# Two more chunks attended in 64x64 quarters, and the first group's FFN2 placed ahead of the third group's FFN1

## The chip, the core and the metric

The kernel runs on one core of a Trainium2 chip. Its engines each work through a queue of their own: TensorE (PE; its weight loads are shown as PEld), VectorE (DVE), ScalarE (ACT), GpSimd (POOL) and SyncE (SP), which here only issues DMAs; GpSimd issues some too. The metric is the device time of one execution in microseconds; before and after are compared by the median of several runs.

## The reference, cut to what matters

Two stages. The first is an mLSTM cell over 4 batches x 8 heads, 768 steps, head size 40, written as a recurrence:

```python
m_new = maximum(f[t] + m, i[t]);  f_stab = exp(f[t] + m - m_new);  i_stab = exp(i[t] - m_new)
C = f_stab * C + i_stab * outer(v[t], k[t])      # per batch and head, 40 x 40
n = f_stab * n + i_stab * k[t]
y[t] = sigmoid(o[t]) * (C @ q[t]) / maximum(abs(n . q[t]), 1.0)
```

The second is a feed-forward layer on the 3072 tokens, each of 8 x 40 = 320 numbers: `relu(x @ w_in)**2 @ w_out`, with w_in 320 x 2048 and w_out 2048 x 320. The weights come as 64-bit floats and are turned into 32-bit ones in the kernel. All arithmetic is 32-bit floating point.

## The kernel before, in words

**Tiling.** The sequence of each batch is cut into 6 chunks of 128 steps; the 24 chunks of the four batches are counted through as s = 0 to 23, so chunks 0 to 5 are batch 0. Within a chunk the recurrence is written as attention: scores of 128 keys against 128 queries for 8 heads, weighted by exp(A + b), where A (broadcast from DRAM into `A_bc`) and b come from the gates. Between chunks a state C per head pair is carried on (`C_old` for the first chunks, `C_b` after). Two chunks make a group g of 256 tokens for the feed-forward layer: FFN1 gives 2048 hidden rows (`g2`), FFN2 the 320 outputs.

**Two forms of attention.** `attend` (L609) uses full 128x128 tiles: the products `hi` (old state), `dC` (new state) and `hp` (values), then `normalise` (L805), then `turn_rows` (L843), which transposes the result on TensorE into `xT`, the FFN's input. `attend_begin` (L684) and `attend_end` (L743) use 64x64 quarters of the array: `values_of_C` (L702), `values_of_P` (L717), `new_C` (L732). Between the halves stands a marker: a VectorE instruction on one element (L700) that waits for the first half on TensorE and for which the second half's `new_C` (or `values_of_C`) waits in turn. The quarter form gives its numerators transposed; they are turned in 32x32 blocks on VectorE (L758), stored to DRAM (`store_num`, `num_rows`), loaded rearranged (`load_num`), normalised (`normalise_turned`, L783), stored (`store_rows`, `x_rows`), loaded (`load_rows`) and turned by VectorE into `xT` (`turn_squares`, L838). It also needs the queries scaled by exp(A): `decays` (L480) on ScalarE and `scale_q` (L669) on VectorE.

The constants `KQ_SQ, X_SQ, ROT = 7, 6, 8` (L339) say from which chunk on the keys and queries are loaded in squares (`load_squares`, `turn_kq`), from which on x goes by DRAM, and from which on heads and keys are rotated.

**Order.** Everything is written out by hand; each engine works in the order of the program. First comes a prologue with the gates and chunks 0 and 1. Then a loop over u = 0 to 7 (L1228) does, on even u, scores and FFN1 quarters, and on odd u `attend(s)` for s = 2 to 5, the transposes of the next chunk, and another FFN1 quarter. Quarters 0 to 3 are FFN1 of group 0, quarters 4 to 7 of group 1. In between, `rounding` converts 18 pieces of the weights: `words` on ScalarE, `join` on VectorE with a last sum on GpSimd (L240), after which SP fetches the next raw piece. Pieces 0 to 9 are w_in, 10 to 17 w_out.

Then comes the main loop over `parts` (L1317), four parts n to a chunk from s = 6 on. In each set of four, part at = 0 has the scores, at = 1 `attend_begin`, the scores of the next chunk or FFN rows, `attend_end`, the stores and loads; at = 2 and 3 the steps on the next chunk. Each part carries a piece of FFN1 (which = 1: `ffn1_open`, `ffn1_rows`, `ffn1_close`, which trade multiplications for sums on VectorE, among them `xs`, `sums_of_x`, L1028) or FFN2 (which = 2). The parts begin with FFN1 of group 2 (`ffn1_begin`, L1046), then FFN2 of group 0 (`ffn2`, L906, four parts), then FFN2 of group 1, FFN1 of group 3, and so on; sums of w_out (`sums_of_weights`, T0 to T3, L935 to L946) serve the FFN2 of later groups (`ffn2_fast`).

PSUM: `ps_at` has 3 banks; in the u loop `ps_h` has 3 and `ps_o` 2, later `ps_h` has all 5.

Of the kernel before, what the change touches and what calls it, by code (L numbers as in the profile page):

```python
# [29 lines left out]
def kernel(  # L30
# [80 lines left out]
    bdm = conv.tile([P, PR, 2, D1], F32, bufs=1)  # L111
# [13 lines left out]
    def make_consts():  # L125
# [24 lines left out]
        nc.gpsimd.memset(bdm[:], 1.0)  # L150
        nc.gpsimd.memset(bdm[:DP, :, 1, :], 0.0)
        nc.gpsimd.memset(bdm[DP:, :, 0, :], 0.0)
# [186 lines left out]
    KQ_SQ, X_SQ, ROT = 7, 6, 8  # L339
# [22 lines left out]
    def load_k(s):  # L362
# [3 lines left out]
        eng = nc.sync if s < 10 else nc.gpsimd  # L366
# [4 lines left out]
    def load_v(s):  # L371
# [3 lines left out]
        eng = nc.sync if s < 10 else nc.gpsimd  # L375
# [88 lines left out]

    def mask(s):
# [14 lines left out]
    def decays(s):  # L480

        if s % NB > 0:
            e = st[s]["eA"] = kq_b[2 + s % 2][:, 1].rearrange("p (j two) d -> p j (two d)", two=2)
# [10 lines left out]
    def weigh(s, masked=False, part=None, vw=True):  # L494
# [4 lines left out]
        if s < X_SQ and part != 1:  # L499
            d["dec"] = prep.tile([P, H], F32, name="dec")  # L500
# [7 lines left out]
        for i in (range(len(A) if s < ROT else 0) if part is None else (part,)):  # L508
# [5 lines left out]
            if s < X_SQ:  # L514
                nc.scalar.activation(d["dec"][:, hh], A[i][:, :, P - 1], AF.Exp)
# [83 lines left out]
    C_old = []  # L599

    def decay_old(s):
        if s + 1 < NB:
            Cd = st[s]["Cd"] = old.tile([P, PR, 2, D1], F32, name="Cd", bufs=1)
            nc.gpsimd.tensor_tensor(
                Cd[:].rearrange("p j i d -> p (j i) d"), C_old[(s - 1) % 2][:].rearrange("p j i d -> p (j i) d"),
                st[s]["dec"][:].unsqueeze(2).to_broadcast([P, H, D1]), op=ALU.mult,
            )

    def attend(s):  # L609
# [41 lines left out]
        if c > 0:  # L651
            num = d["num"] = old.tile([P, H, D1], F32, name="num", bufs=1)
            nc.vector.tensor_tensor(
                num[:], hi[:], eA_T[:, b, c, :].unsqueeze(2).to_broadcast([P, H, D1]), op=ALU.mult,
# [3 lines left out]
        if c + 1 < NB:  # L658
            Cn = C_old[s % 2]
            if c == 0:  # L660
                nc.vector.tensor_tensor(Cn[:], dC[:], bdm[:], op=ALU.mult)
# [12 lines left out]
    def decay_C(s):  # L674
        if s % NB > 0:
            Cd = st[s]["Cd"] = attn.tile([P, PR, D1], F32, name="Cd", bufs=1)
            nc.gpsimd.tensor_tensor(
                Cd[:], C_b[(s - 1) % 2][:, : PR * D1].rearrange("p (j d) -> p j d", d=D1),
# [3 lines left out]
    LIVE = [slice(DP * i, DP * i + D) for i in range(2)]  # L682

    def attend_begin(s):  # L684
# [13 lines left out]
        else:  # L698
            end, spare = out[1][DP : DP + 1, P : P + 1], C_b[(s - 1) % 2][0:1, 4 * D1 : 4 * D1 + 1]
        nc.vector.tensor_scalar(spare, end, scalar1=0.0, scalar2=None, op0=ALU.mult)  # L700

    def values_of_C(s, rows, order=(0, 1)):  # L702
        d = st[s]
        C = C_b[(s - 1) % 2]
        for e in order:
            for m in order:
                i, j = rows[m], 2 * m + e
                nc.tensor.matmul(  # L708
                    d["numT"][m][HALVES[e], i, :], lhsT=C[LIVE[i], j * D1 : j * D1 + DP], rhs=d["eA"][LIVE[i], j, :],
# [33 lines left out]
    def attend_end(s):  # L743
# [11 lines left out]
        tn = attn.tile([P, P // SQ, PR, SQ], F32, name="tn", bufs=1)  # L755
        to = tn[:].rearrange("p m c r -> p c m r")
# [3 lines left out]
        if c + 1 < NB:  # L760
            Cn = C_b[s % 2][:, : PR * D1].rearrange("p (m x) -> p m x", m=2)
            for m in range(2):
                dC = d["out"][m][:, 2 * P : 2 * P + 2 * D1]
                if c > 0:
                    nc.vector.tensor_tensor(
                        Cn[:, m], dC, d["Cd"][:].rearrange("p (m e) d -> p m (e d)", m=2)[:, m], op=ALU.add,
# [5 lines left out]
    def store_num(s):  # L772
        nc.sync.dma_start(n_d[s], st[s]["tn"][:].rearrange("p m j r -> p (m j r)"))

    def load_num(s):
        N = st[s]["N"] = kq_b[s % 2][:, 1].rearrange("p h d -> p (h d)")
# [28 lines left out]
    def normalise(s):  # L805
        d = st[s]
        num = d["num"]
        if num is not d["hp"]:
            nc.vector.tensor_tensor(num[:], num[:], d["hp"][:], op=ALU.add)
# [96 lines left out]
    def ffn2(g, j, part):  # L906
        if part == 0:
            st["o_ps"] = ps_h.tile([P, W], F32, name="h_ps")[:, :DM]
        o_ps = st["o_ps"]
# [136 lines left out]
    def ffn1_begin(g):  # L1046
        new_g2(g)
        xT = st["xT", g]
        begun = st["begun"] = [
            (ps_h.tile([P, 4, P], F32, name="h_ps"), ffn.tile([P, 4, P], F32, name="r_sb", bufs=4)) for _ in range(2)  # L1050
        ]
        for q, (X, m1) in enumerate(begun):
            blocks(X, F11, xT[:, 0, 0, :], q, True)
# [407 lines left out]
```

## Time and profile before

| | |
|---|---|
| median of 3 runs | 490.53 us (490.36 to 493.19) |
| the profiled execution | 491.22 us, span 489.4 us, mean granted clock 0.999 |
| TensorE busy | 481.7 us of the span (98%) |
| VectorE, ScalarE, GpSimd busy | 341.8, 240.4, 215.3 us |
| moved by DMA | 68.08 MB, mean 139 GB/s |
| u loop ends, main loop's first FFN starts | 90.99 us |
| scores of chunk 8 start | 130.02 us |

The times inside the execution are counted from the start of the span. A line of a timeline has the start, the duration, the engine, the line of the kernel, the operation, the tile written and the tiles read, and in brackets how long the engine sat idle before it and what ended that. Matmul durations overlap, so distances between starts are the measure. A line of the waits says who waited for whom, how long in total, how often, and the longest.

### The profile page before, as it was taken

The numbers are of one execution on the slowest core, as the hardware profiler recorded it, in microseconds if no ns is written. First come the engines' busy times: TensorE is split into PE (matmuls) and PEld (weight loads), VectorE is DVE, ScalarE is ACT, GpSimd is POOL, SyncE is SP. The second block draws the span as 40 slices with busy tenths as digits, with TensorE's granted clock in tenths as the row PEclk, the third lists the DMA queues.
The fourth block names the chain that finished last, engine by engine and source line by source line (L and its number), as shares of the span: only waits on it lengthen the run. The fifth ranks groups of instructions, "written<-read, shape, count | busy, mean of one in ns | idle before, by whom it ended". The sixth has DMA issues, their size and how long they took to land.

```text
span 489.4 us, 15237 instructions
## 1 busy us (share of the span) xinstructions
PE 481.7 (98%) x6169; PEld 449.0 (92%) x6169; DVE 341.8 (70%) x704; ACT 240.4 (49%) x531; POOL 215.3 (44%) x322
## 2 busy tenths in 40 slices
PE   9999999999999999999999999999999999999997
PEld 4886788897799999999999999999999999999996
DVE  7799767888946856957966956857856956635441
ACT  4676996764522650942742941742942640513300
POOL 6455533432679178078179078078174040020000
PEclk9999999999999999999999999999999999999999
DMA  9999997745878579758759778658665612200000
GB/s 185 227 243 227 304 230 183 151 84 140 171 130 199 120 138 225 134 107 212 135 99 219 140 117 208 134 109 213 123 106 129 149 51 82 55 28 2 3 27 29
DMA packets 191096, 68.08 MB, mean 139 GB/s; under 512 B 158833, under 2 KB 180241, under 8 KB 191025
## 3 DMA queue, kind: packets, MB, share of 16 engines
q1 hardware_dynamic: 185280, 57.50, 55.1%
q0 software_dynamic: 5600, 9.50, 8.1%
q8 instruction: 49, 0.80, 0.7%
q14 instruction: 23, 0.18, 0.1%
q10 hardware_dynamic: 144, 0.10, 0.1%
HBM read 54.77 MB, written 18.01 MB: 149 GB/s over the span
## 4 chain that ended last, share of the span: by engine, by line
PE 87%; ACT 5%; SPq 4%; DMA 3%; issue 1%; DVE 0%; ACTq 0%
PE h_ps L965 35%; PE h_ps L1041 26%; PE h_ps L1090 8%; PE h_ps L911 4%; PE h_ps L874 3%; PE numT L727 3%; PE numT L708 2%; DMA lent_t<-in_moe_w_in_dram 1%; PE numT L738 1%; SPq L210 1%; PE tp L575 1%; PE h_ps L575 1%; SPq L1151 1%; ACT g_c L511 1%; DMA raw<-in_moe_w_in_dram 1%; DMA og<-in_o_gate_dram 1%
## 5 line engine op out<-in xcount | busy, mean ns | idle before, releaser
L475 POOL TENSOR_SCALAR_AFFINE_SELECT A_bc<-A_bc 64x512 f32<-64x512 f32 x32 | 22.5, 704 | 80.4 <-ACT kq L492 57.9
L965 PE MATMUL h_ps<-T,S 128*128 128x160 f32 x352 | 51.7, 300 | 0.6 <-ACT g_c L1107 0.6
L1071 ACT COPY r_sb<-h_ps 128x512 f32<-128x512 f32 x18 | 10.5, 585 | 84.2 <-PE h_ps L1041 84.2
L965 PEld LDWEIGHTS h_ps<-T,S 128*128 128x128 f32 x352 | 48.9, 190 | 1.1 <-ACT g_c L1107 0.9
L965 PE MATMUL h_ps<-w_out,g 128*128 128x160 f32 x336 | 49.2, 303 | 0.0
L981 DVE TENSOR_TENSOR y_sb<-y_sb,h_ps 128x160 f32<-128x160 f32 x44 | 14.1, 320 | 47.7 <-PE h_ps L965 47.6
L965 PEld LDWEIGHTS h_ps<-w_out,g 128*128 128x128 f32 x336 | 46.1, 190 | 1.3 <-issue 0.5
L1041 PE MATMUL h_ps<-xT,w_in 128*128 128x128 f32 x320 | 42.8, 278 | 0.0
L1041 PE MATMUL h_ps<-lent_t,w_in 128*128 128x128 f32 x320 | 42.2, 275 | 0.0
L1041 PEld LDWEIGHTS h_ps<-xT,w_in 128*128 128x128 f32 x320 | 38.9, 192 | 1.4 <-issue 1.0
L1090 PE MATMUL h_ps<-xT,w_in 64*64 64x128 f32 x960 | 39.1, 272 | 0.0
L1041 PEld LDWEIGHTS h_ps<-lent_t,w_in 128*128 128x128 f32 x320 | 38.9, 192 | 0.2 <-issue 0.2
L1041 PE MATMUL h_ps<-lent_t 128*128 128x128 f32 x320 | 39.0, 275 | 0.0
L1041 PEld LDWEIGHTS h_ps<-lent_t 128*128 128x128 f32 x320 | 37.3, 192 | 0.0
L505 ACT ACTIVATE A_bc<-A_bc,b_R 128x64 f32<-128x64 f32 (+1 forms) x128 | 35.7, 361 | 1.8 <-POOL A_bc L475 1.4
L1090 PEld LDWEIGHTS h_ps<-xT,w_in 64*64 64x64 f32 x960 | 34.8, 133 | 1.3
L379 POOL DMA_DIRECT2D va<-in_v_dram x56 | 34.2, 619 | 1.8 <-DMA kq_rows<-in_q_dram 1.3
L758 DVE STREAM_TRANSPOSE tn<-numT 128x256 f32<-128x256 f32 x36 | 14.0, 428 | 28.5 <-PE numT L708 19.2
L874 PE MATMUL h_ps<-xT,w_in 128*128 128x256 f32 x128 | 30.1, 385 | 1.6 <-ACT xT L853 1.2
L874 PEld LDWEIGHTS h_ps<-xT,w_in 128*128 128x128 f32 x128 | 23.4, 190 | 6.1 <-POOL w_in L240 1.6
L1033 POOL TENSOR_TENSOR lent_t<-xT 128x128 f32<-128x128 f32 (+1 forms) x18 | 14.6, 833 | 32.7 <-DVE xT L840 32.7
L965 PE MATMUL h_ps<-w_out,g_c 128*128 128x160 f32 x192 | 28.0, 302 | 0.0
(218 smaller groups left out, 1150.0 us busy)
## 6 DMA issues: line engine op xcount, KB each, us to landing
A_bc<-a_slots SPq DMA_DIRECT2D x32, 256.0 KB, 4.4
num_rows<-tn SPq DMA_DIRECT2D x18, 256.0 KB, 2.3
kq<-num_rows SPq DMA_DIRECT2D x72, 64.0 KB, 2.1
raw<-in_moe_w_out_dram SPq DMA_DIRECT2D x7, 640.0 KB, 5.4
kqT<-kq_rows SPq DMA_DIRECT2D x34, 128.0 KB, 3.3
og<-in_o_gate_dram SPq DMA_DIRECT2D x24, 160.0 KB, 4.9
out_dram<-y_sb SPq DMA_DIRECT2D x24, 160.0 KB, 3.1
raw<-in_moe_w_in_dram SPq DMA_DIRECT2D x7, 512.0 KB, 6.9
```

What stands on the lines that cost most here:

```text
L379: eng.dma_start(dst[HALVES[n], PR * (1 - late_keys) : PR * (2 - late_keys)], src[HALVES[late_keys], PR * m : PR * (m + 1)],)
L475: nc.gpsimd.affine_select(part, part, compare_op=ALU.is_ge, fill=-1e30, base=0, pattern=[[0, PR], [0, 2], [1, DP]], channel_multiplier=-1,)
L505: nc.scalar.activation(A[0][:, x, to], A[0][:, x, to], AF.Exp, bias=b_R[:, b, c, own, x : x + 1],)
L727: nc.tensor.matmul(d["numT"][m][HALVES[e], i, t0:], lhsT=va_w[s % NKQ][keys, at * D1 : at * D1 + DP], rhs=rhs, start=(s % NB == 0 and i == ...
L758: nc.vector.transpose(to[:, 2 * m : 2 * m + 2], d["numT"][m].rearrange("p c t -> p (c t)"))
L874: nc.tensor.matmul(hs[i][:, n, :], lhsT=w_in[:, a, fb * P : (fb + 1) * P], rhs=xT[:, :, a, :], start=(n == 0 and a == 0), stop=False,)
L911: nc.tensor.matmul(o_ps, lhsT=st["g2", g][:, fb, j * P : (j + 1) * P], rhs=w_out[:, fb, :], start=(fb == 0), stop=(fb == NF - 1),)
L965: nc.tensor.matmul(to, lhsT=lhsT[:, p], rhs=rhs[:, p, :], start=(start and p == 0), stop=(p == NPAIR - 1), skip_group_check=True,)
L981: add = lambda to, a, b: nc.vector.tensor_tensor(to, a, b, op=ALU.add)
L1033: sub = lambda to, a, b: eng.tensor_tensor(to, a, b, op=ALU.subtract)
L1041: nc.tensor.matmul(to[:, n, :], lhsT=lhsT[:, 4 * q + n, :], rhs=rhs, start=(start and n == 0), stop=True, skip_group_check=True,)
L1090: nc.tensor.matmul(to[cols, n, :], lhsT=w_in2[rows, 4 * q + n, cols], rhs=rhs, start=(start and n == 0), stop=True, skip_group_check=True,)
```

## The change

Chunks 4 and 5 (the fifth and sixth) go over to the quarter form: `X_SQ` becomes 4. So they have no `turn_rows`, their numerators and rows go by DRAM, and their state is kept so that both forms can read it (`C_flat` holds it; `state(s)` chooses). Their queries are scaled by `decays` and `scale_q`, which need A unmasked: for them the mask is not put on A but as a fill of zeros on W = exp(A + b) (`mask_W`). Chunk 4's exp and decays stand ahead of the weight conversion on ScalarE at u = 2. Their two attention halves follow each other directly, at u = 5 and u = 7. `load_num(4)` is issued behind `load_k(8)` and ahead of `load_v(8)`; `load_num(5)` behind `load_squares(7)`. Chunk 4 is normalised at the end of u = 7, chunk 5 at n = 0.

In the main loop FFN2 of group 0 comes first, both first halves ahead of both second halves, and FFN1 of group 2 second, in the form that all later groups have; `ffn1_begin` goes. The last two weight pieces are converted at n = 0 and 1, scores(7) stand between the halves of chunk 6, and chunk 9's k and v are loaded by GpSimd. The sums of w_out move to n = 2 to 4, those of group 1 to n = 4 and 6.

```diff
-    KQ_SQ, X_SQ, ROT = 7, 6, 8
+    KQ_SQ, X_SQ, ROT = 7, 4, 8
...
-        eng = nc.sync if s < 10 else nc.gpsimd
+        eng = nc.sync if s < 9 else nc.gpsimd
...
+    def mask_W(s):
+        nc.gpsimd.affine_select(
+            st[s]["W"], st[s]["W"], compare_op=ALU.is_ge, fill=0.0, base=0, pattern=[[0, H], [1, P]],
+            channel_multiplier=-1,
+        )
...
-            e = st[s]["eA"] = kq_b[2 + s % 2][:, 1].rearrange("p (j two) d -> p j (two d)", two=2)
+            home = kq_b[2 + s % 2 if s >= NB else s - X_SQ - 1]
+            e = st[s]["eA"] = home[:, 1].rearrange("p (j two) d -> p j (two d)", two=2)
...
+            if s >= X_SQ:
+                st[s]["Cd"] = Cd = Cd[:].rearrange("p j i d -> p (j i d)")[:, : PR * D1].rearrange("p (j d) -> p j d", d=D1)
+                for i, rows in enumerate(HALVES):
+                    nc.gpsimd.tensor_tensor(
+                        Cd[rows], C_old[(s - 1) % 2][rows, :, i, :],
+                        st[s]["dec"][rows, i::2].unsqueeze(2).to_broadcast([DP, PR, D1]), op=ALU.mult,
+                    )
+                return
...
-            if c == 0:
-                nc.vector.tensor_tensor(Cn[:], dC[:], bdm[:], op=ALU.mult)
+            for i in range(2 if c == 0 else 0):
+                nc.vector.tensor_copy(Cn[HALVES[i], :, i, :], dC[HALVES[i], :, i, :])
...
+    def state(s):
+        return (C_b if s >= NB else C_flat)[s % 2]
...
-        C = C_b[(s - 1) % 2]
+        C = state(s - 1)
...
-        N = st[s]["N"] = kq_b[s % 2][:, 1].rearrange("p h d -> p (h d)")
+        N = st[s]["N"] = kq_b[s % 2 if s >= NB else s - X_SQ - 1][:, 1].rearrange("p h d -> p (h d)")
...
-    def ffn1_begin(g):
...
     # u loop, even u
-                turn_rows(s - 1)
+                if s - 1 < X_SQ:
+                    turn_rows(s - 1)
                 scores(s)
                 ffn1(u // 4, u % 4)
             if u == 2:
+                weigh(4, masked=True, vw=False)
+                decays(4)
                 rounding.words()
             weighted(s)
...
             if u == 2:
-                mask(s + 1)
                 rounding.join()
+                mask_W(4)
                 rounding.join()
-                weigh(s + 1, masked=True)
+                values(4)
                 rounding.words()
             else:
-                weigh(s + 1, masked=(u == 0), vw=(u > 0))
+                weigh(s + 1, masked=(u != 6), vw=(u == 6))
+                if u == 4:
+                    mask_W(5)
                 square_half()
+                if u > 0:
+                    scale_q(s)
     # u loop, odd u
-            attend(s)
+            if s < X_SQ:
+                attend(s)
+            else:
+                attend_begin(s)
+                attend_end(s)
...
-            normalise(s)
+            if s < X_SQ:
+                normalise(s)
+            else:
+                store_num(s)
...
-            for r in {5: (8,), 7: (9,)}.get(u, ()):
-                load(r)
-            for r in {5: (7,), 7: (8,)}.get(u, ()):
-                pair_up(r)
+            if u == 5:
+                load_k(8)
+                load_num(4)
+                pair_up(7)
+                load_v(8)
+            if u == 7:
+                load_squares(7)
+                load_num(5)
+                pair_up(8)
...
+            if u == 5:
+                decays(5)
+            if u == 7:
+                normalise_turned(4)
+                store_rows(4)
...
-    turn_rows(5)
-    load_squares(7)
...
     # main loop
-    parts = [(1, 2, i) for i in range(4)] + [(2, 0, i) for i in range(4)]
-    for g in range(1, NG):
+    parts = []
+    for g in range(NG):
         parts += [(2, g, i) for i in range(4)]
...
-    LAST = (17, 17, 17, 17, 18)
+    ROUNDED = (17, 18)
...
+        if n == 0:
+            turn_kq(7)
+            load_rows(4)
+            normalise_turned(5)
+            store_rows(5)
...
             do(store_num, s)
+            if n == 1:
+                load_rows(5)
+                turn_squares(4)
             do(load_num, s)
...
-            ffn2(g, *divmod(i, 2))
+            ffn2(g, i % 2, i // 2)
...
+        if n == 3:
+            load(9)
...
+        for x in {2: (0,), 3: (1, 2), 4: (3,)}.get(n, ()):
+            sums_of_weights(x)
+        if n in (4, 6):
+            sums(1, slice(0, NPAIR), (n // 2 - 1,))
```

## The prediction

> **What bounds the kernel now.** I read the page's engine table first, then the chain that ended last, then TensorE's own waits after the first 60 us, then the timelines around the change.
>
> ```profile
> PE 481.7 (98%) x6169; PEld 449.0 (92%) x6169; DVE 341.8 (70%) x704; ACT 240.4 (49%) x531; POOL 215.3 (44%) x322
> ...
> PE 87%; ACT 5%; SPq 4%; DMA 3%; issue 1%; DVE 0%; ACTq 0%
> ```
>
> TensorE is the bound, and the chain runs over it for 87% of the span. The next view is TensorE's waits from 60 us to the end (total, times, longest):
>
> ```profile
> PE h_ps L874 <- ACT xT L853: 1.2, 1, 1.2
> PE h_ps L965 <- ACT g_c L1107: 0.6, 1, 0.6
> PE numT L738 <- DVE kq L700: 0.3, 1, 0.3
> ```
>
> Only 2.1 us of waiting in 430 us. So each microsecond of TensorE work taken out after 60 us is worth a microsecond, and each new wait there costs one. How near VectorE is, by stretch (TensorE, weight loads, VectorE, ScalarE, GpSimd busy; clock; DMA share; GB/s):
>
> ```profile
> 61.00:91.00 30.00, 30.00 (x213) 24.83 (x211) 21.81 (x36) 24.95 (x50) 10.51 (x7) 1.00 0.91 200
> 91.00:130.00 39.00, 38.72 (x482) 32.24 (x480) 33.32 (x66) 23.48 (x51) 15.79 (x23) 1.00 0.60 124
> 130.00:200.00 70.00, 70.00 (x1046) 68.56 (x1046) 48.19 (x103) 26.57 (x66) 45.36 (x73) 1.00 0.76 160
> ```
>
> From 91 to 130 us VectorE is busy 85% of the time, the highest of the three; the change puts more into just this stretch. The work that goes and its substitute, from TensorE's timeline (start, duration; the ends overlap, so I cost by the distance from start to start):
>
> ```profile
> 65.28 1.12 PE L622 MATMUL hi<-Co,kqT 128*128 128x82 f32 x8
> 66.24 1.06 PE L634 MATMUL dC<-vw,kq 128*128 128x82 f32 x8
> 67.13 1.92 PE L645 MATMUL hp<-va,g_c 128*128 128x41 f32 x16
> 68.87 1.07 PE L549 MATMUL tp<-ident,kq 128*128 128x128 f32 x8
> ...
> 74.39 0.44 PE L848 MATMUL tp<-ident,x_sb 128*128 128x128 f32 x2
> 74.76 0.44 PE L850 MATMUL tp<-ident,x_sb 128*64 128x128 f32 x4
> 75.13 1.16 PE L583 MATMUL tp<-kqT 40*128 40x128 f32 x16
> ...
> 114.47 0.45 PE L708 MATMUL numT<-kq,C 40*64 40x128 f32 x8
> ...
> 115.85 0.44 PE L738 MATMUL numT<-vw,kq 64*64 64x41 f32 x16 [0.28 <-DVE kq L700]
> ...
> 116.90 13.19 PE L911 MATMUL h_ps<-w_out,g 128*128 128x320 f32 x48
> ```
>
> And ScalarE ahead of the one wait at 60 us:
>
> ```profile
> 44.17 0.48 ACT L853 COPY xT<-tp 128x384 f32<-128x384 f32 x1
> 48.93 0.68 ACT L220 ACTIVATE mag<-raw 128x512 f32<-128x512 f32 x1 [4.27 <-DMA raw<-in_moe_w_in_dram]
> ...
> 50.08 2.43 ACT L511 ACTIVATE g_c<-A_bc,b_T 128x128 f32<-128x128 f32 x8
> ...
> 60.00 0.51 ACT L853 COPY xT<-tp 128x384 f32<-128x384 f32 x1
> ```
>
> [...] chunk 7's whole attention in quarters takes 116.90 - 114.47 = 2.43 us, chunk 4's in full tiles 68.87 - 65.28 = 3.59. [...] ScalarE sits 4.27 us before L220 although L511 behind it needs no weights. My stalls rest on this. [...] Here the 256 KB `num_rows` stores landed after 2.0 to 2.3 us, x_rows stores after 2.9 to 3.5.
>
> **The change part by part: what it saves.** Chunk numbers are the code's s (4 and 5 are the change's fifth and sixth).
> - Attention of chunk 4: 3.59 - 2.43 = 1.16. Chunk 5, last of its batch, has no new state: full 83.64 - 80.94 = 2.70; quarters 2.43 less the two L738 stretches (0.39 + 0.25) = 1.79; saves 0.91. Each quarter form keeps the 0.28 bubble, since nothing stands between its halves.
> - `turn_rows` of 4 and 5 goes: 75.13 - 74.39 = 0.74 each, 1.48.
> - Chunk 7's bubble (0.28) goes: FFN rows now stand between its halves.
> - FFN work is only reordered: 0.
> - ScalarE: exp(A) of chunk 4 (2.43, plus 0.20 for dec) and the new `decays(4)` (two of 0.62) stand ahead of the conversion that waits until 48.93. A(4) was issued at 35.33 and landed 8.9 later, 44.2; so they run from 44.65 to 48.5, inside the 4.27 us of idling. The next conversion needs a raw piece issued at 45.28 that landed 6.0 later, at 51.3, against its 52.52 now. Followed down the queue, the xT copy ends 59.5 instead of 60.5, and TensorE starts group 1 at 59.55, not 60.56: 1.0. (Its own limit is 59.40. If the landing slips, 0.3.)
> Sum: 1.16 + 0.91 + 1.48 + 0.28 + 1.0 = 4.8 us. The masks by fill, plain copies instead of the 0/1 product and halved Cd lie beside TensorE: 0. ScalarE gains about 1 us in 61 to 86 (decays(5), two more half-tanh copies, less two xT copies); my walk down its queue leaves 0.7 us before the nearest PSUM release, so 0; without that cover, up to 1.
>
> **What it costs.** TensorE's times after the change, by the starts above: group 1 from 59.55, attention(5) ends 79.8, scores(6) end 86.4, FFN2(0) first quarter to 90.9 (4.50), begin(6) 91.6, scores(7) 92.6. Then four waits.
> (a) end(6) needs the tiny VectorE marker behind begin(6). Behind attention(5) VectorE must do: transposes 0.71, join 1.79, normalise_turned(4) 1.84 (107.70 to 109.54), join 1.79, sum L1026 1.2, weighted(6) 1.21, turn_kq(7) 1.2, normalise_turned(5) 1.84, join 1.79, marker 0.16 = 13.5: 93.35, already 0.75 late. And turn_kq(7) waits for its load: SP frees raw at 82.3 behind a join, stores num(5), then issues the four squares in 3.41 (as at 94.15), last landing 89.6, where VectorE wanted 88.4: 1.25 more. load_num(5), behind them, lands 90.7 and is just in time. Stall 2.0.
> (b) FFN2's last weight piece. SP after load_num(5) (88.2): pair_up(8) 2.5, og 1.2, store_rows(4) at 91.9, landing 3.2, load_rows(4) 1.85, landed 98.7. VectorE's turn_squares(4) stands ahead of w_in's sum and the last join: 98.7 + 0.5 + 1.2 + 1.8, GpSimd's add 1.54: 103.8. TensorE wants it at 94.6 + 0.8 + 4.37 + 3.28 = 103.05. Stall 0.8. The first output token tile then ends at E = 104.9.
> (c) FFN1(2) needs xs. At n=2 ScalarE's y copy (0.43) waits for E and weigh(7) (2.45) stands behind it; then VectorE: weighted(7) 1.21, normalise_turned(6) 1.84, T0 1.45, xs up to its third row 0.85: E + 8.2. TensorE is there after 4.37 + 0.9: E + 5.3. Stall 3.0. In the kernel before weigh(7) waited for its mask only.
> (d) end(7)'s marker: from there VectorE has xs 0.3, T1 and T2 2.9, U2 and U4 1.3, L946 1.4, S1 1.25, marker 0.15 = 7.3; TensorE 2.7 + 1.1 + 1.77 = 5.5. Stall 1.8.
> Behind it VectorE has about 3 us of slack to group 1's FFN2, so nothing is passed on. GpSimd takes the loads of chunk 9 (seven of 0.6 to 0.8), ahead of mask(8): that mask waits for decays(8) until about 114 anyway, so 0. The out stores and pair_up(9) on SP stand before num(7): 0.
> Stalls 2.0 + 0.8 + 3.0 + 1.8 = 7.6; net 7.6 - 4.8 = **2.8 us slower**. The profiled execution took 491.22 (span 489.4): 494.0. The median of the runs is 490.53, 0.7 lower: **493.3**.
>
> **Bounds of the unknown.** DMA landings under the new load are not in the trace. Low end: no DMA wait at all leaves (a) 0.75 and (b) 0, together 5.5: +0.7. High end: load_rows landings as at 130.87 (5.9 instead of 2.2): (b) is 3.7 longer: +6.5. I take landings as measured in 94 to 115, where the DMA share was near 0.6.
>
> **Rivals.**
> - *The waits don't reach TensorE (faster).* One mechanism: VectorE keeps up, as its 70% suggests, and the 4.8 us stay: 490.5 - 4.8 = 485.7. It decides from where (c) falls under 1.5 us, half of it: then the net is near zero and (d) shrinks too. For it: TensorE waited 2.1 us in 430. Against: the 85% of 91 to 130, into which two normalisations, two transposes and eight FFN sums are moved.
> - *SP's queue is the new bound (more slower).* The landing of the high end: 497.
> - *Quarters save nothing here,* because nothing stands between their halves, so each costs as much as the full form: gain 2.8, net 4.8: 495.3. Against: 2.43 was measured with the bubble.
>
> **How the numbers follow.** Forecast 0.55 (491 to 496), first rival 0.22 (485 to 490), second 0.18 (496 to 499), third 0.05. The range leaves about a tenth at each end: 486.5 to 497.5; the likeliest case alone 491.2 to 496. One per cent, about what a measurement of this kernel can tell from no change, is 4.9 us: under 485.6 lies a third of the first rival, 0.08; over 495.4 the second and part of the forecast and of the third, 0.28; between 0.64.
>
> **What would show it.** Right: group 1's first FFN1 at about 59.5; no L848 after chunk 3; scores(6) ending near 86.4; TensorE's waits naming VectorE's marker twice, GpSimd's w_out once and the xs sums once, with 7 to 8 us in all; scores(8) about 3 us later than 130.02; nothing new behind that. Wrong: scores(8) near 125, or a wait of which I have no word, such as PSUM banks released by ScalarE between 61 and 86.

## The result and the profile after

The changed kernel takes 509.35 us (median of 4 runs, 508.21 to 512.18) against 490.84 (490.36 to 493.19): ratio 1.0376, 95% interval 1.0327 to 1.0424. The prediction said 493.3 us, +2.8; the sign was right, the size less than a sixth. The profiled execution took 508.37 us, its span 506.6. A number in brackets behind a step is its chunk or group: scores(6) are those of chunk 6, FFN2(0) is FFN2 of group 0.

The page's engine table and its chain that ended last, after:

```profile
PE 484.6 (96%) x6229; PEld 449.7 (89%) x6229; DVE 340.2 (67%) x719; ACT 242.3 (48%) x534; POOL 222.4 (44%) x328
...
PE 76%; ACT 6%; DMA 6%; DVE 5%; SPq 4%; issue 2%; POOL 1%; DVEq 0%; ACTq 0%; POOLq 0%
```

TensorE's busy time *rose* by 2.9 us although work was taken from it, and the chain leaves it more often: 76% instead of 87%. By stretch (the columns are as in the prediction), after:

```profile
61.00:91.00 30.00, 25.70 (x271) 21.03 (x269) 20.86 (x42) 23.84 (x49) 13.95 (x9) 1.00 0.81 185
91.00:130.00 39.00, 29.56 (x187) 21.30 (x188) 20.56 (x44) 11.66 (x28) 13.37 (x19) 0.82 0.64 142
130.00:200.00 70.00, 68.65 (x1105) 66.17 (x1104) 50.93 (x107) 34.91 (x79) 38.98 (x61) 1.00 0.67 137
```

In 91 to 130 us every engine does less than before: VectorE is busy for 53%, not 85%. So the stretch isn't short of an engine; the engines wait for each other and for transfers. The granted clock there is 0.82. TensorE's four longest waits from 60 us on, after (total, times, longest):

```profile
PE h_ps L933 <- issue: 5.6, 1, 5.6
PE h_ps L1063 <- DVE lent_t L1058: 5.1, 1, 5.1
PE numT L757 <- DVE kq L718: 2.7, 3, 2.3
PE h_ps L987 <- issue: 0.8, 1, 0.8
```

And where they lie, on TensorE's timeline (start, duration, in brackets the idle time before and its releaser):

```profile
86.19 1.06 PE L587 MATMUL tp<-kqT 40*128 40x128 f32 x16
92.80 7.47 PE L933 MATMUL h_ps<-w_out,g 128*128 128x320 f32 x16 [5.56 <-issue]
...
100.90 1.08 PE L579 MATMUL h_ps<-kqT 40*64 40x128 f32 x32
104.28 0.44 PE L757 MATMUL numT<-vw,kq 64*64 64x41 f32 x16 [2.30 <-DVE kq L718]
...
114.87 5.65 PE L933 MATMUL h_ps<-w_out,g 128*128 128x320 f32 x20 [0.27 <-POOL w_out L236]
...
126.49 3.44 PE L1063 MATMUL h_ps<-lent_t 128*128 128x128 f32 x16 [5.07 <-DVE lent_t L1058]
```

The same two steps on TensorE's timeline before:

```profile
89.90 1.16 PE L583 MATMUL tp<-kqT 40*128 40x128 f32 x16
...
109.97 4.57 PE L911 MATMUL h_ps<-w_out,g 128*128 128x320 f32 x16
```

The first line of each shows the saving: scores(6) start at 86.19 us, where they started at 89.90 before. FFN2(0) should follow at once and comes 5.56 us later. "issue" hides the releaser. ScalarE's timeline shows it:

```profile
90.29 0.78 ACT L216 ACTIVATE mag<-raw 128x640 f32<-128x640 f32 x1 [5.45 <-DMA raw<-in_moe_w_out_dram]
90.97 0.75 ACT L218 ACTIVATE low<-raw 128x640 f32<-128x640 uint32 x1
91.64 1.07 ACT L920 ACTIVATE g<-h_ps 128x512 f32<-128x512 f32 x2
```

And SyncE's queue of DMA issues (start, time to issue):

```profile
76.08 2.57 SPq L800 DMA_DIRECT2D kq<-num_rows  x4
...
85.31 0.81 SPq L206 DMA_DIRECT2D raw<-in_moe_w_out_dram  x1
...
87.15 0.84 SPq L795 DMA_DIRECT2D num_rows<-num  x1
88.08 7.54 SPq L398 DMA_DIRECT2D kqT<-kq_rows  x4
95.73 3.02 SPq L800 DMA_DIRECT2D kq<-num_rows  x4
```

The raw piece at 85.31 was issued at 79.90 before:

```profile
79.90 0.37 SPq L210 DMA_DIRECT2D raw<-in_moe_w_out_dram  x1
```

The relu of FFN1(1) (L920), whose PSUM banks FFN2(0) gets, stands on ScalarE behind words of w_out (L216) that wait for this piece. Ahead of it SyncE stood from 73.4 to 76.08 for chunk 4's stored numerators and issued their loads for 2.57 us: together 5.2 us, as against 5.4 us of delay. The same queue brings kqT(7) and chunk 5's numerators; VectorE, after:

```profile
98.02 1.25 DVE L405 STREAM_TRANSPOSE kqT<-kqT 128x1024 f32<-128x1024 f32 x1 [7.47 <-DMA kqT<-kq_rows]
100.29 0.17 DVE L812 TENSOR_SCALAR dm<-kq 128x8 f32<-128x8 f32 x1 [1.02 <-DMA kq<-num_rows]
...
104.07 0.16 DVE L718 TENSOR_SCALAR kq<-numT 1x1 f32<-1x1 f32 x1
```

The last view is TensorE's clock (the third number from the end) in two slices of 2 us behind its waits:

```profile
94.00:96.00 2.00, 2.00 (x5) 1.35 (x4) 0.00 (x0) 1.38 (x3) 0.45 (x2) 0.50 0.74 106
...
106.00:108.00 2.00, 2.00 (x5) 1.28 (x4) 0.29 (x3) 0.00 (x0) 1.20 (x2) 0.50 0.32 52
```

FFN2(0)'s first 16 matmuls take 7.47 us, where 16 such took 4.57 before. An estimate of what this cost is TensorE's busy time times (1 - clock), summed over the slices from 92 to 130 us: 6.1 us, of which 3.0 behind the first wait, 1.7 behind the second, 1.5 behind the wait of 5.07. Balance at the start of scores(8) (145.74, before 130.02, +15.7): -3.7 of TensorE work (what scores(6) gained), +13.4 of waits (5.56, 2.30, 0.27, 5.07, 0.15) less the 0.3 there was, +6.1 of clock: 15.5. Another 1.5 comes behind it, 0.8 of it the fourth wait in the list (L987); the rest I did not trace.

### The profile page after: what moved, and what is told of

Read it like the earlier page. It is cut to its first block, busy times and chain, and to the rows that moved or that the text cites. A ratio compares the mean times of both kernels' runs of the same rounds, so it can differ in the third digit from the quotient of the medians.

```text
span 506.6 us, 15402 instructions
## 1 busy us (share of the span) xinstructions
PE 484.6 (96%) x6229; PEld 449.7 (89%) x6229; DVE 340.2 (67%) x719; ACT 242.3 (48%) x534; POOL 222.4 (44%) x328
## 4 chain that ended last, share of the span: by engine, by line
PE 76%; ACT 6%; DMA 6%; DVE 5%; SPq 4%; issue 2%; POOL 1%; DVEq 0%; ACTq 0%; POOLq 0%
PE h_ps L987 34%; PE h_ps L1063 25%; PE h_ps L1096 7%; PE numT L746 2%; PE numT L727 2%; DMA lent_t<-in_moe_w_in_dram 2%; SPq L398 1%; DMA raw<-in_moe_w_out_dram 1%; PE numT L757 1%; PE idle L1145 1%; ACT g_c L515 1%; PE h_ps L579 1%; PE tp L579 1%; DMA num_rows<-num 1%; SPq L800 1%
## 5 line engine op out<-in xcount | busy, mean ns | idle before, releaser
L478 POOL TENSOR_SCALAR_AFFINE_SELECT A_bc<-A_bc 64x512 f32<-64x512 f32 x32 | 23.8, 743 | 83.5 <-ACT kq L496 56.7
L1077 ACT COPY r_sb<-h_ps 128x512 f32<-128x512 f32 x20 | 11.7, 586 | 86.3 <-PE h_ps L1063 86.3
L987 PE MATMUL h_ps<-T,S 128*128 128x160 f32 x352 | 51.8, 300 | 0.0
L987 PE MATMUL h_ps<-w_out,g 128*128 128x160 f32 x336 | 49.4, 303 | 0.8 <-issue 0.8
L987 PEld LDWEIGHTS h_ps<-T,S 128*128 128x128 f32 x352 | 48.9, 190 | 0.5 <-ACT g_c L1112 0.3
L987 PEld LDWEIGHTS h_ps<-w_out,g 128*128 128x128 f32 x336 | 46.1, 190 | 2.4 <-issue 1.8
L1063 PE MATMUL h_ps<-lent_t 128*128 128x128 f32 x320 | 40.5, 281 | 5.1 <-DVE lent_t L1058 5.1
L1063 PEld LDWEIGHTS h_ps<-lent_t 128*128 128x128 f32 x320 | 38.7, 198 | 5.2 <-issue 5.2
L375 POOL DMA_DIRECT2D va<-in_v_dram x60 | 36.8, 619 | 4.0 <-DMA kq_rows<-in_k_dram 1.7
L933 PE MATMUL h_ps<-w_out,g 128*128 128x320 f32 x64 | 22.6, 520 | 5.8 <-issue 5.6
```

The source lines that it names most:

```text
L375: eng.dma_start(dst[HALVES[n], PR * (1 - late_keys) : PR * (2 - late_keys)], src[HALVES[late_keys], PR * m : PR * (m + 1)],)
L478: nc.gpsimd.affine_select(part, part, compare_op=ALU.is_ge, fill=-1e30, base=0, pattern=[[0, PR], [0, 2], [1, DP]], channel_multiplier=-1,)
L933: nc.tensor.matmul(o_ps, lhsT=st["g2", g][:, fb, j * P : (j + 1) * P], rhs=w_out[:, fb, :], start=(fb == 0), stop=(fb == NF - 1),)
L987: nc.tensor.matmul(to, lhsT=lhsT[:, p], rhs=rhs[:, p, :], start=(start and p == 0), stop=(p == NPAIR - 1), skip_group_check=True,)
L1063: nc.tensor.matmul(to[:, n, :], lhsT=lhsT[:, 4 * q + n, :], rhs=rhs, start=(start and n == 0), stop=True, skip_group_check=True,)
L1077: nc.scalar.copy(m1[:], X[:])
```

## The experiments

Theory A, from the profile as it stands: each wait is worth its own length and the clock behind it. Theory B: the waits are where TensorE meets one chain (SyncE's queue, then VectorE), so taking one away uncovers the next. The times below are ratios to the kernel before on the same chip; the changed kernel's is 1.0376.

**ScalarE's order: the relu ahead of the waiting words.**

```diff
+        if u == 7:
+            relu_half()
+            square_half()
         while rounding.done < NEXT[u]:
             rounding.step()
```

> ScalarE's relu of group 1's last FFN1 quarter is put ahead of the w_out words that wait for a late transfer, so TensorE's idle stretch of 5.56 us before FFN2(0) should shrink to about 1.2 us (last FFN1 matmul ends 87.2, two relus of 0.5 us each). Theory A (every idle stretch of the profile after is worth its own length and the half clock behind it): 5.56 - 1.2 = 4.4 us and about 2.5 of the 2.9 us of half clock come back, 509.4 - 6.9 = 502.5 us. Theory B (a chain SyncE's queue, kqT of chunk 7, VectorE, marker of chunk 6 holds the second half of attention(6) at 104.3 us whatever TensorE does before it): FFN2(0) starts at about 88.4, and a new wait of some 6 to 7 us opens before scores(7), which needs kqT turned (99.3 us); attention(6)'s second half starts at 104.3 as before: 509.4, within 1 us.

1.0336 (1.0294 to 1.0377), not told apart from the changed kernel. TensorE's timeline:

```profile
86.42 4.54 PE L933 MATMUL h_ps<-w_out,g 128*128 128x320 f32 x16 [0.32 <-issue]
99.24 2.08 PE L579 MATMUL h_ps<-kqT 40*64 40x128 f32 x32 [7.47 <-DVE dm L812]
103.03 0.66 PE L757 MATMUL numT<-vw,kq 64*64 64x41 f32 x16 [1.71 <-DVE kq L718]
```

The first wait is gone and FFN2(0) runs 6.4 us sooner (this run was 1.15 us ahead at scores(6) already), at full clock. Then TensorE waits 7.47 us for kqT(7), which VectorE turns at 97.94. The second half of attention(6) starts 1.25 us earlier than in the changed kernel. Theory A said -6.9; B is right here. (The releaser is named as the next VectorE instruction, L812; the turn L405 ends as it starts.)

**The raw piece ahead of chunk 4's numerators.** `load_num(4)` is put behind the rounding loop of the same step.

> The load of chunk 4's numerators, which stood in SyncE's queue from 73.4 to 78.65 us, is put behind the fetch of the next piece of w_out, so that fetch is issued at about 80 instead of 85.3 us, and its words reach ScalarE in time. Theory A: TensorE's idle stretch before FFN2(0) falls from 5.56 to about 1.2 us, and most of the half clock behind it goes: about 502.5 us. Theory B: SyncE's queue gains only the 2.7 us for which it stood waiting for the stored numerators, so kqT of chunk 7 lands at about 95.5 instead of 98, the marker of chunk 6 comes at about 101.5 instead of 104.1, and the time falls by those 2.7 us, to about 506.7. If the words were late by the transfer's own length and not by its place in the queue, nothing changes: 509.4.

1.0288 (1.0254 to 1.0321). The edit missed its aim: the late piece is fetched a step later in the code, so it was still issued at 85.31. The median, 506.84 us, is what theory B had said, but by luck: B's step was kqT(7) at 95.5, and it was turned at 97.44. By the ratios some 4 us came back, by the spans of the two profiles 1.7; where they came from I did not trace. The run shows something else. In this profile TensorE reached scores(6) at 88.30, 2.1 us later than in the changed kernel, and FFN2(0) still started at 92.52, its wait shrunk to 3.16: the restart is set by the transfer, not by when TensorE gets there.

**Chunk 5 normalised behind the marker of chunk 6.**

```diff
         if n == 0:
             turn_kq(7)
             load_rows(4)
-            normalise_turned(5)
-            store_rows(5)
         if at == 1:
             do(attend_begin, s)
+            if n == 1:
+                normalise_turned(5)
+                store_rows(5)
```

> VectorE's normalising of chunk 5 (with the store of its rows) is put behind the marker of chunk 6. VectorE then has the turn of kqT(7) to 99.3 and one piece of rounding (1.8 us) ahead of the marker: 101.2 us, before TensorE's first half ends at 102. Both theories: the 2.30 us wait goes, and with it the stretch at half clock in 105 to 110 us, 1.7 us of lost clock: 509.4 - 4.0 = 505.4 us under A; B says the same or the 2.3 alone (507.1) if the clock falls anyhow.

1.0323 (1.0297 to 1.035), not told apart from the changed kernel. TensorE's timeline:

```profile
100.96 0.44 PE L757 MATMUL numT<-vw,kq 64*64 64x41 f32 x16 [0.30 <-DVE kq L718]
...
114.53 8.29 PE L933 MATMUL h_ps<-w_out,g 128*128 128x320 f32 x20 [4.94 <-POOL w_out L236]
```

The 2.30 us wait falls to 0.30, and the wait for the last w_out piece grows from 0.27 to 4.94: VectorE joins that piece only behind the turn of chunk 4's rows, which come over SyncE's queue and were turned at 109.39 (109.73 in the changed kernel). Both theories had forecast a fall of 2.3 to 4 us here, and both missed. What happened, one wait gone and the next uncovered, is B's picture, but B was not on record with it for this run.

**Chunk 7's weights ahead of FFN2's copy, w_out's first sum behind the sums of x.**

```diff
+        if n == 2:
+            do(lambda s: weigh(s, masked=True), s + 1)
         if fast:
 ...
         if at == 2:
-            do(lambda s: weigh(s, masked=True), s + 1)
+            if n != 2:
+                do(lambda s: weigh(s, masked=True), s + 1)
 ...
-        for x in {2: (0,), 3: (1, 2), 4: (3,)}.get(n, ()):
+        for x in {3: (0, 1, 2), 4: (3,)}.get(n, ()):
```

> ScalarE's weights of chunk 7 are put ahead of the copy of FFN2's first output (for which ScalarE had waited 19 us until 116.25), and the first sum of w_out's blocks (1.48 us) behind the sums of x on VectorE. The products of chunk 7 and the normalising of chunk 6 then run while TensorE is still in FFN2, and the sums of x of group 2 are there at about 121.4 us, when TensorE has done its first block. The 5.07 us wait before FFN1(2)'s second block falls to under 1 us, and the 1.5 us lost to the half clock behind it too: about 503 us. If this wait only hides another that ends as late (turned rows of chunks 4 and 5, weights' sums), the time stays at 509.4.

1.0223 (1.019 to 1.0257), some 7 us back; the span fell by 6.3. ScalarE's timeline shows why the wait was one of order:

```profile
107.02 2.44 ACT L515 ACTIVATE A_bc<-A_bc,b_T 128x128 f32<-128x128 f32 x8 [9.74 <-POOL A_bc L472]
115.94 0.42 ACT L939 COPY y_sb<-h_ps 128x320 f32<-128x320 f32 x1 [6.48 <-PE h_ps L933]
```

And in the changed kernel:

```profile
116.25 0.43 ACT L939 COPY y_sb<-h_ps 128x320 f32<-128x320 f32 x1 [19.01 <-PE h_ps L933]
```

The weights (L515) need only the mask (L472). In the changed kernel they ran at 116.70, behind the copy. Here theory A's price holds: the wait of 5.07 us and the half clock behind it went, and the time fell by about as much. Of the four waits on the timeline above, this alone came from ScalarE's order without SyncE's queue.

**SyncE's queue shortened.** Chunk 8's loads, pairs and the last two gates are issued behind chunk 5's numerators; chunk 4's numerators are loaded behind the pairs of chunk 7 and the gates, once they have been stored.

```diff
             if u == 5:
-                load_k(8)
-                load_num(4)
                 pair_up(7)
-                load_v(8)
             if u == 7:
                 load_squares(7)
                 load_num(5)
-                pair_up(8)
-            if u > 4:
+            if u == 5:
                 load_o(2 * s)
                 load_o(2 * s + 1)
+                load_num(4)
 ...
                 normalise_turned(4)
                 store_rows(4)
+                load_k(8)
+                load_v(8)
+                pair_up(8)
+                load_o(2 * s)
+                load_o(2 * s + 1)
```

> Only SyncE's order changes: the loads of chunk 8 (k, v, pairs) and of the second two output gates are issued after the numerators of chunk 5, and chunk 4's numerators are loaded after the pairs of chunk 7, when they have been stored. Some 4 us of issues and 2.7 us of standing leave the queue ahead of kqT of chunk 7. Theory B (SyncE's queue sets when kqT(7), the numerators of chunk 5 and the late piece of w_out come, and TensorE's waits from 87 to 105 us are only the places where it meets them): the late piece is fetched at about 80 to 82 instead of 85.3, FFN2(0) starts at about 88.5 instead of 92.8 at full clock, kqT(7) lands at 91 to 94 instead of 98, the marker of chunk 6 comes at about 98, and attention(6) ends some 6 us earlier. The wait of 5.07 us before FFN1(2)'s second block is untouched, because ScalarE's weights of chunk 7 stand behind FFN2's copy: 509.4 - 6 = 503.4 us (501 to 506). Theory A (ScalarE's order): the marker stays at 104 us and the time within 1 us of 509.4.

1.0247 (1.0208 to 1.0285), about 6 us back by the ratios, 4.6 by the spans of the profiles, as theory B had said. TensorE's timeline:

```profile
87.71 4.54 PE L933 MATMUL h_ps<-w_out,g 128*128 128x320 f32 x16 [0.46 <-issue]
...
99.00 0.67 PE L757 MATMUL numT<-vw,kq 64*64 64x41 f32 x16 [4.96 <-DVE kq L718]
```

And VectorE's:

```profile
91.54 1.25 DVE L405 STREAM_TRANSPOSE kqT<-kqT 128x1024 f32<-128x1024 f32 x1 [0.98 <-DMA kqT<-kq_rows]
94.84 0.17 DVE L812 TENSOR_SCALAR dm<-kq 128x8 f32<-128x8 f32 x1 [2.06 <-DMA kq<-num_rows]
```

Nothing on ScalarE was touched, yet the wait before FFN2(0) is down to 0.46, and kqT(7) is turned at 91.54, 6.5 us sooner. Either edit, the relu's or the queue's, takes the first wait away; only the queue's also brings kqT(7) sooner. So ScalarE's order was where the first wait stood, and SyncE's queue where it came from. The 4.96 us left are the marker behind chunk 5's normalising and a join.

**TensorE kept busy in the holes.** Matmuls of zeros, which nothing reads, at three places (`fill(pool, tag, n)` issues n of them; its definition is left out).

```diff
+    fill(ps_at, "at", 22)
     banks.close()
 ...
+                if n == 1:
+                    fill(ps_h, "h_ps", 8)
 ...
+        if g == 2 and q == 0:
+            fill(ps_h, "h_ps", 20)
```

> The kernel after with TensorE kept busy by matmuls of zeros (bf16, 128x512, nothing reads them) in three idle stretches: 22 before FFN2(0), 8 before the second half of attention(6), 20 before FFN1(2)'s second block. Theory: the half clock follows idling, so the granted clock stays at 1.00 from 92 to 100, 105 to 110 and 126 to 130 us, FFN2(0)'s first 16 matmuls take 4.6 instead of 7.5 us; what each part gains before a wait that ends at a fixed time is lost in that wait, so only the last stretch's 1.5 us and part of the second's 1.7 come back: 506.5 to 508. Rival (the clock falls for another reason, such as the transfers then running): the clock column is at 0.50 in the same places and the time at 509.4 or above.

1.0294 (1.0248 to 1.0339), as the theory had said, and not told apart from the changed kernel; its span is 2.1 us shorter. The clock column is 1.00 for 61 to 91, 91 to 130 (0.82 in the changed kernel) and 130 to 200 us, as in this slice:

```profile
94.00:96.00 2.00, 2.00 (x10) 1.37 (x8) 0.00 (x0) 2.00 (x4) 0.45 (x2) 1.00 1.07 156
```

TensorE's timeline:

```profile
86.57 4.99 PE L1147 MATMUL idle<-zeros 128*128 128x512 bf16 x22
91.49 1.16 PE L587 MATMUL tp<-kqT 40*128 40x128 f32 x16
93.23 4.54 PE L933 MATMUL h_ps<-w_out,g 128*128 128x320 f32 x16 [0.58 <-issue]
...
103.85 0.44 PE L757 MATMUL numT<-vw,kq 64*64 64x41 f32 x16 [1.45 <-DVE kq L718]
```

So here the half clock follows TensorE's idling and not the transfers, which in this slice are no less busy (1.07) than in the changed kernel (0.74). FFN2(0) is 2.9 us shorter, but the second half of attention(6) starts at 103.85, only 0.43 us sooner: what the clock gains before a wait with a fixed end is lost in it. The gain behind the third hole was lost at the next marker (1.55 us): scores(8) start at 145.60, against 145.74.

**The order of the parts alone.** The kernel before, with the changed kernel's order of parts and places of sums; chunks 4 and 5 as before, none of the new transfers.

```diff
-    parts = [(1, 2, i) for i in range(4)] + [(2, 0, i) for i in range(4)]
-    for g in range(1, NG):
+    parts = []
+    for g in range(NG):
         parts += [(2, g, i) for i in range(4)]
 ...
```

> The kernel before with the change's order of the parts alone (FFN2(0) ahead of FFN1(2), FFN1(2) in the order of the other groups, the sums placed as in the changed kernel, chunk 7's scores inside chunk 6's section); chunks 4 and 5 attended, normalised and turned as before, with none of the new transfers. If the order is what costs (it asks for kqT of chunk 7 at about 97 us, where the kernel before needed it at 109 and had it landed at about 101, and for ScalarE's weights of chunk 7 behind FFN2's copy): waits of about 5 us before scores(7) and 5 us before FFN1(2)'s second block, 3 us of half clock behind them: 491 + 13 = 504 us (499 to 508). If the new transfers on SyncE's queue are what costs, this order runs within 3 us of the kernel before: 491 to 494 us.

1.0293 (1.0264 to 1.0322): 14.4 us slower by itself, as the first of the two forecasts had said. TensorE's timeline:

```profile
101.39 2.08 PE L575 MATMUL h_ps<-kqT 40*64 40x128 f32 x32 [4.61 <-DVE kqT L409]
...
124.71 3.76 PE L1041 MATMUL h_ps<-lent_t 128*128 128x128 f32 x16 [4.99 <-DVE lent_t L1036]
```

Two waits, 9.6 us, and 5.4 us of half clock behind them (summed as above), make up the +14.8 at scores(8). kqT(7) is no later than it was. VectorE turned it here at 100.09, as soon as it had landed:

```profile
100.09 1.25 DVE L409 STREAM_TRANSPOSE kqT<-kqT 128x1024 f32<-128x1024 f32 x1 [7.31 <-DMA kqT<-kq_rows]
```

The kernel before turned it at 105.72 and used it at 108.98:

```profile
105.72 1.23 DVE L409 STREAM_TRANSPOSE kqT<-kqT 128x1024 f32<-128x1024 f32 x1
...
108.98 1.05 PE L575 MATMUL tp<-kqT 40*64 40x128 f32 x32
```

The new order asks for kqT(7) at 96.8, 12 us sooner, since FFN1(2) no longer stands ahead. The second wait is the one of ScalarE's order: chunk 7's weights behind FFN2's copy. The change's other half saves 3.7 us of TensorE work and adds transfers to the very queue the new order made urgent; together they end 4 us above the order alone by the ratios, 1.1 by the spans of the profiles. No run has the quarters and their transfers in the old order, so what that half does by itself is known only from this difference.

**Mending everything.** Relu, marker, weights and short queue together, and the last w_out piece behind the marker:

> SyncE's shorter queue as in the run of that order alone; the relu ahead of the w_out words; chunk 5's normalising behind the marker of chunk 6, and the last piece of w_out right behind that marker; ScalarE's weights of chunk 7 ahead of FFN2's copy and the first sum of w_out's blocks behind the sums of x. If the four waits (13.1 us) and the half clock behind them (6.1 us) are all that the change cost, up to 19 us come back: 490.2, and with 1 to 3 us of waits left over 491 to 493 us; with all of the chunk products' saving kept (3.8 us) it cannot be under 487. If the 64x64 quarters or the new order of the parts cost something by themselves, it stays at 497 us or more.

1.016 (1.0118 to 1.0202). The first three waits are nearly gone, but the one for the sums of x is there with 7.40 us, now because chunk 5's rows stood on SyncE behind chunk 8's loads. I followed the wait from place to place.

Chunk 8's loads put around the row transfers, the sums of x right behind the turned rows:

> As the mended kernel before it, which still waited 7.40 us for the sums of x of group 2 (VectorE turned chunk 5's rows only at 112.07 us, because SyncE's queue held chunk 8's loads, 9.5 us of issues, between the store and the load of chunk 4's rows, and chunk 5's rows stood behind those). Here chunk 8's loads stand around the row transfers and not ahead of them, chunk 5 is normalised ahead of the last piece of w_out, the sums of x follow the turn of chunk 5's rows at once, and the first sum of group 1's activations stands behind the marker of chunk 7. Theory (all of the loss is SyncE's queue and the order on ScalarE and VectorE behind it): rows of chunk 5 turned at about 108, sums of x by 109.5, TensorE's wait there 0 to 1 us, no half clock; 500.1 - 7.4 - 3.0 - 1.0 = 488.7 us, 487 to 492, within 0.7% of the kernel before. If something else in the new order costs (the quarters, the parts' order), a wait of as much turns up elsewhere and the time stays at 496 us or more.

1.0151 (1.0114 to 1.0187): 2.95 us left there, 5.11 behind three sums of w_out on VectorE.

Those sums into VectorE's idle stretch, chunk 5's rows stored ahead of the pairs:

> The mended kernel before this one lost its gain to two waits on VectorE: 5.11 us for the first sum of FFN1(2), behind three sums of w_out's blocks (4.8 us), and 2.95 us for the sums of x of group 2, because chunk 5's rows, ready at 99.2 us, were stored at 102.1 behind pairs and gates. Here the three sums stand in VectorE's idle stretch of 8.5 us before chunk 5's rows, and those rows are stored ahead of the pairs. Theory (every wait of the change is one of order on VectorE, ScalarE and SyncE): both waits fall under 1 us and no stretch of half clock (2.9 us) is left before 140 us: 500.1 - 5.1 - 2.9 - 2.9 + 1 = about 490 us, 487 to 493. If the new order of the parts has no place for VectorE's work between 100 and 140 us, a wait of some 4 to 5 us turns up at a third place and the time stays at 495 to 500 us.

1.0095 (1.0059 to 1.013): no wait over 2.1 us.

Chunk 6 normalised behind FFN1(2)'s first sums, two other sums moved:

> As the mended kernel before it, whose TensorE still waited 2.08 us for FFN1(2)'s first sum behind chunk 6's normalising on VectorE, 0.41 us for chunk 7's marker behind a sum of w_out's blocks, and 1.13 us for the weighted scores of chunk 8 behind group 1's second sum. Chunk 6 is normalised behind FFN1(2)'s first two sums, and the two other sums stand in VectorE's idle 2.85 us at 130 us. Theory: 3.6 us less, 496.1 - 3.6 = 492.5 us (491 to 494), level with the kernel before within what is measured: the change's 3.8 us of saved TensorE work is eaten by short waits that its order brings. If the quarters cost something by themselves beyond these waits, it stays at 496 us; if all waits go, it could reach 488.

1.0077 (1.0049 to 1.0105), 495.32 us, the lowest, though not told apart from the one before it. Its one long wait, on TensorE's timeline:

```profile
129.30 1.75 PE L1063 MATMUL h_ps<-lent_t,w_in 128*128 128x128 f32 x8 [4.48 <-DVE r_sb L1079]
```

VectorE stood 3.83 us for chunk 6's rows, stored later by this edit. Their turn moved behind FFN1(2)'s next sums:

> The mended kernel before this one had one long wait of TensorE left, 4.48 us at 124.8 us: chunk 6's rows, normalised later by that very edit, were turned on VectorE at 126.96 us ahead of FFN1(2)'s third sum. Here they are turned behind that sum and the next. Theory: the wait and the half clock behind it (1.7 us) go: 495.3 - 6.2 = 489.1 us (488 to 492), level with the kernel before or 0.5% under it; the chunk products' 3.8 us cannot come back whole, since some 3 us of short waits stay between 88 and 116 us. If the wait turns up elsewhere once more, 494 to 496 us.

1.0134 (1.009 to 1.0177): 3.71 us before chunk 8's values, behind chunk 7's normalising. That moved too:

> The mended kernel before this one had one long wait left, 3.71 us at 135.3 us: the weighted scores of chunk 8 on VectorE, behind chunk 7's normalising, which waits until 133.07 us for its numerators whatever stands before it, and the half clock behind that wait cost 4 us more. Here chunk 7 is normalised behind the weighted scores of chunk 8. Theory: 499.1 - 3.7 - 5 = 490.4 us (488.5 to 492.5), level with the kernel before (491.2 to 492.1 in these series) or up to 0.7% under it. Against: a wait of about as much turns up at a next place, 494 to 497 us.

1.0164 (1.0126 to 1.0202): 4.29 us at the same place, now for kqT(9), which SyncE had issued at 132.15 behind chunk 7's numerators. kqT(9) first:

> The mended kernel before this one still waited 4.29 us for chunk 8's weighted scores, on VectorE behind the turn of kqT(9), whose load stood on SyncE's queue behind the numerators of chunk 7 (a stand of 4.1 us until they were stored). Here kqT(9) is loaded first. Theory (SyncE's queue again): 500.4 - 3.8 - 4.5 of half clock = about 492 us (490 to 495). If another transfer or sum takes its place as before, 496 to 500 us.

1.0112 (1.0072 to 1.0151): that wait 0.31, a marker's 1.90, half clock again behind it. None of the seven beats the kernel before. Each of the seven forecasts lay between 487 and 495 us, level with it or nearly, and each was missed: the medians are 495.3 to 500.4. The best gives back 14.7 of the 18.5 us (by the ratios); whether an order of the queues exists that keeps the 3.7 us of TensorE work stays open.

## Why the prediction was wrong

Up to scores(8) the prediction forecast +2.8 us, and +15.7 came. Of the difference 5.8 us are waits (7.6 forecast, 13.4 measured), 6.1 the clock, and about 0.8 a saving that did not come.

- **TensorE's saving**: scores(6) were to end at 86.4 and end at 87.25. The quarters and the missing `turn_rows` gave within 0.2 us what was said (attention(4) 2.43 us, attention(5) 1.98 instead of 1.79). The 1.0 us from ScalarE's order was 0.1: the weights did run early, but the next raw piece landed late and the words behind it began at 52.40, not sooner than the 52.52 before. The prediction had named this case and put it at 0.3.
- **The step that failed**: "SP frees raw at 82.3 ... last landing 89.6". SyncE issued that raw at 86.72, the four kqT loads took 7.54 us to issue and not 3.41, and kqT(7) was there at 98.0: 8.4 us late. About 4.4 of it is the queue ahead, 4.1 the issue of the four loads. The walk of that queue left out the stand for chunk 4's numerators and the load behind it (5.2 us). I had priced two landings and not the queue ahead of them. With that queue shortened the raw was issued at 83.49, the loads took 4.46 and kqT(7) was turned at 91.54. The same lateness of the queue made the wait before FFN2(0).
- **No wait was forecast before FFN2(0)**; "ScalarE gains about 1 us ... so 0" looked at durations between 61 and 86 us. There the words of a late piece stood in front of a relu: 5.56 us. The last paragraph's "PSUM banks released by ScalarE" was the right name. That ScalarE's later work stands behind a waiting instruction the prediction had read off the 4.27 us ahead of L220, but it used this only at the place where it helped; here the relu (L920) stood behind L216's wait of 5.45 us.
- (a) 2.0, measured 2.30; (b) 0.8, measured 0.27; (d) 1.8, measured 0.15. What agrees here does so by chance, since all three stood behind a TensorE that was already late. In runs where an edit let one of them show, (b) was 4.94 us, (a) 4.96 and (d) 1.27 (marker, short queue, weights).
- (c) 3.0, measured 5.07. The mechanism was the one described, and putting ScalarE's weights first removed it. Mis-sized: weighted(7) also waited for GpSimd's `vw` (0.9 us behind the weights), and the sums up to their third row took 1.85 us, not 0.85.
- **The clock** had no term: by the estimate above 6.1 us, a third of the loss. It came with the waits; holding it at 1.00 alone gave back 2.1 us of the span.
- **The rivals**: "SP's queue is the new bound" had the right queue at 0.18, but counted one transfer (+3.7). The first rival fell: the waits did reach TensorE. The third fell: the quarters saved what they should, with nothing between their halves.
- **"FFN work is only reordered: 0"** holds for TensorE's work, and waits of the new order were priced in (a) to (d). They were priced too low: 7.6 us for the whole change, where the order alone costs 14.4, since it moves the hour at which things are due: kqT(7) to 12 us sooner, and chunk 7's weights behind a copy.

## What to carry to other kernels

This reordering added no work to TensorE and cost 14.4 us, in waits for what feeds it and in the clock behind them. For each transfer of a new order compare its landing with its *new* first use, before costing any instruction. Walk the DMA-issuing queue as you would an engine, with its stands for semaphores (2.7 us here, for chunk 4's numerators), and look at what is queued behind each waiting instruction. A wait in a profile is the first place where a chain is met; until an experiment removes it and the time falls, its length is not known to be its price: 5.56 us taken away gave back nothing that could be told apart, 5.07 us gave back 7.

## What the runs showed of the hardware

The granted clock fell to 0.50 around TensorE's waits and was still low after the work had resumed. In the changed kernel TensorE resumed at 92.80 us, and the slices of 2 us from 92 to 98 show 0.50, the next one 0.82; it resumed again at 104.28, and the slices from 106 to 110 show 0.50 and 0.76. The length of a wait alone did not decide it: the clock fell around waits as short as 1.19 us (the run with chunk 4's numerators moved, where 16 FFN1 matmuls then took 5.38 instead of 3.72 us, and the clock was 0.94 over 61 to 91 us) and 2.30 us (the 0.50 from 106 us on), and did not around another of 1.19 us (the mended kernel that follows the lowest, 3.72 us for the same matmuls, clock 1.00) and one of 2.95 us (mended, chunk 8's loads put around the row transfers, where the 16 FFN1 matmuls behind it took 2.02 us; in the changed kernel, behind 5.07 us, they took 3.44). What else decides it, no run here shows. With bf16 matmuls of zeros in the waits the clock was 1.00 over 91 to 130 us, where it was 0.82 without them.

The four kqT loads of a chunk took 2.3 to 8.4 us to issue on SyncE. Those of chunk 7 took 6.8 to 8.4 us in the six runs in which two raw pieces of 640 KB were issued less than 2 us apart right ahead of them, 4.4 to 4.6 in the eight in which these were about 4 us apart, and 3.4 in the two (the kernel before and the order alone) in which other loads stood between. Why, no run here isolates.
